# A pre-norm attention and gated-MLP layer on one Trainium2 core: other block choices, another order at the tail

## The chip, the core and the metric

The kernel runs on one core of one Trainium2 chip. A core has a matrix engine (TensorE, in the profile PE, its weight loads PEld), a vector engine (VectorE, DVE), a scalar engine for activation functions (ScalarE, ACT), a general engine (GpSimd, POOL) and a queue that issues transfers (SyncE, SP). Each runs its own instruction stream and they meet through semaphores. The time is device microseconds of one execution. Five runs of the kernel before gave a median of 750.84 us, from 750.54 to 751.12.

## The reference

All tensors are bfloat16; the sequence has 2048 rows of 512.

```python
B, S, D, H = 1, 2048, 512, 32          # Dh = 16, F = 1792
qkv = layernorm(x) @ wqkv              # q, k, v of 32 heads
p = softmax(q @ k.T * 16 ** -0.5)      # per head, 2048 x 2048
h = x + (p @ v) @ wo
g, u = layernorm(h) @ w_gate, layernorm(h) @ w_up
out = h + (sigmoid(g) * u) @ w_down
```

With 16 columns a head, the exponentials (32 x 2048 x 2048) weigh as much as the matmuls.

## The kernel before, in words

**Attention.** A unit is 128 x 512 scores of one head: 256 query columns against two tiles of 128 keys (512 columns against one tile in the first two blocks). The array is used in four parts of 32 rows for the scores, one for each head row j, so that up to four heads are multiplied side by side (`scores`, L1087). A tile is usually three units in three PSUM banks. ScalarE takes the exponential of two or three units in one instruction (L1415). Where three units are there, VectorE can take the third (`dexp_first`, L1258): it turns the score into the bits of a 16-bit float with one operation, and GpSimd makes two shifted copies (L1279), so that three value products are summed for this unit where ScalarE's needs one. Values are multiplied with 17 columns, the last a constant, so each accumulator row also holds the row sum (`av`, L1235). All value products go to PSUM bank 0 (`acc`). When a group of four heads has had all its keys, `finish_group` lets VectorE transpose the sum (L1153), take reciprocals into `rsum` (L1123), scale (L1124) and, for every second group, transpose back into `ot` (L1129).

**The rest.** Projections, output projection with its layer norm (`wo_ln`), gate and up products (`ffn_up`, L826), the tanh that stands for the sigmoid (L856), their product (L898) and the down projection (`ffn_down`, L844) are generators in a queue `bg`. They are called dense work: one step is two to four matmuls.

**The planner.** The order of instructions on all engines is written out by hand while the program is built. A clock T for each engine is carried along: 216 ns for a matmul of 512 columns (`MM`, L638), 112 ns for each change between scores, value products and dense work (`SWITCH`, L639), 51 + 426.5 ns per unit for an exponential (L1416), 601 ns for one of VectorE (L1260), and tails and latencies (L520, L521). For every tile n the loop issues the scores of the next tile, the exponential of this one, and then fills PE until the clock says that the exponential is through (`lim`, L1431). Each block of the filling is chosen by a rule: a step of dense work if there are tokens for it, else value products of up to 12 units, else one dummy matmul that keeps PE's clock up (`stir`), else 100 ns go by.

`PLAN` (L23) overrides the rule, by the key 16 n + step:

- steps 0 to 13 are the blocks of tile n (L1435). 1, 2 or 3: value products of up to 4, 8 or 12 units. 4: a dense step whatever the tokens. 5: let 100 ns go by. 9: end the tile.
- 14 turns the head row of VectorE's unit (L1035).
- 15 decides the sharing (L1398). 1: ScalarE takes all three units. 2: VectorE takes one even where the clock says that it is late.

**The tail.** After the last tile, one block of 256 query rows is left to finish, in a fixed order: value rows of all earlier tiles; on ScalarE a square root to load its table (L1504); 2 matmuls that put twice x into the two output banks `hps` (L1506) and 6 that add the first three quarters of the output projection (L1509); the weights of the 14 last gate and up products, loaded by SP into the freed `J` tiles (L1519, ten transfers); the last value rows and `finish_group` (L1525); the last quarter of the projection (L1532); the layer norm, with 14 matmuls of down projection left over from the queue beside it (`leftover`, L1551); transposes, 10 more such matmuls; 14 rounds of gate, up, tanh and product (`gate_mm`, `tanh_out`, `glu_out`), where gate and up use two pairs of PSUM banks by turns and all tanh results one buffer `th`; 28 matmuls of down projection (L1584), two copies out (L1587) and two stores (L1588).

**The guard.** The exponentials take no row maximum. So at the end VectorE looks whether all row sums lie in a range (L1593 to L1600), one matmul sums the result over the partitions (L1601), and a cast puts it into `flag` (L1603). All engines load the flag (L1607) and branch (L1608): only if a sum is out of range does `general` do everything again in a safe way.

Of the kernel before, what the change touches and what calls it, by code (L numbers as in the profile page):

```python
# [8 lines left out]
FP32 = mybir.dt.float32  # L9
FP16 = mybir.dt.float16  # L10
BF16 = mybir.dt.bfloat16
I16 = mybir.dt.int16
I32 = mybir.dt.int32
I64 = mybir.dt.int64
ALU = mybir.AluOpType
ACT = mybir.ActivationFunctionType
AX = mybir.AxisListType
# [2 lines left out]
DependencyClass = mybir.DependencyClass  # L20
DependencyReason = mybir.DependencyReason

PLAN = {414: 2, 528: 5, 656: 5, 672: 2, 736: 4, 737: 3, 750: 2, 769: 9, 801: 2, 815: 1, 817: 2, 1198: 3, 1200: 3, 1201: 3, 1376: 1, 1409: 3, 1423: 1, 1472: 9, 1473: 5, 1474: 4, 1601: 9, 1634: 3, 1682: 4, 1696: 9, 1713: 4, 1840: 9, 1857: 5, 1872: 4, 1873: 1, 1890: 9, 1938: 1, 2033: 1, 2047: 1, 2144: 5, 2145: 2, 2161: 2, 2384: 2, 2417: 4, 3728: 3, 3730: 4, 4240: 1, 4255: 1, 4321: 3, 4353: 4, 4367: 2, 4752: 2, 4753: 5, 4767: 2, 6112: 5, 6129: 3, 7040: 3, 7041: 3, 7696: 4, 7711: 1, 7713: 4, 7742: 2, 7761: 9, 7904: 2, 8512: 4, 8513: 3, 8913: 1, 8926: 3, 8928: 2, 8930: 1, 8943: 2, 8944: 4, 8960: 3, 8975: 1, 9200: 3, 9393: 4, 9410: 4, 9889: 4, 9890: 3, 9952: 2, 9984: 3, 10000: 2, 10178: 3, 10302: 2, 10528: 3, 10543: 2, 10640: 1, 10687: 2, 10703: 2, 10848: 4, 10894: 2, 10945: 1, 10959: 2, 11023: 1, 11089: 4, 11102: 1, 11103: 1, 11106: 1}  # L23

LOG2E = 1.4426950408889634

# [6 lines left out]
SUM_LOW, SUM_HIGH = 256.0, 60000.0  # L33
# [111 lines left out]
def kernel(  # L145
# [11 lines left out]
    nc = tc.nc  # L157
    P = 128
    S, D = A_x.shape[1], A_x.shape[2]
# [4 lines left out]
    NG = H // 4  # L164
    NP = NG // 2
# [37 lines left out]
    ident2 = const.tile([P, P], BF16)  # L203
# [13 lines left out]
    wo_sb = const.tile([P, NP, D], BF16)  # L217
    rsum = const.tile([P, S // 32 * NG], FP32)
# [31 lines left out]
    fill = prep.tile([P, QC], BF16, name="fill")  # L250
# [186 lines left out]
    for h in range(2):  # L437
# [11 lines left out]
        out=small.tile([P, 1], FP32, name="warm")[:], in_=eps_t[:], func=ACT.Exp))])  # L449
# [29 lines left out]
    while left:  # L479
        best = None  # L480
        for n in left:
# [11 lines left out]
            for eng, ns, fn in t.opts:  # L493
                start = max(at, free[eng])
# [17 lines left out]
    acc = PS[:, 0, :]  # L512
# [9 lines left out]
    T = {e: max(0.0, free[e] - tasks["go"].end) for e in free if e != "N"}  # L522
# [141 lines left out]
    def pe_time(mode, ns, acts=None):  # L664
        st["acts"].append((T["P"], ns / MM * 512 if acts is None else acts))
        T["P"] += ns + (SWITCH if st["mode"] != mode else 0.0)
        st["mode"] = mode
# [89 lines left out]
    OT, otj = {}, {}  # L757
# [79 lines left out]
    def glu_out(hT, f, th, ps):  # L837
        w = ps.shape[-1]
        nc.vector.scalar_tensor_tensor(out=hT[:, f, 0:w], in0=th[:, 0:w], scalar=1.0, in1=ps,  # L839
                                       op0=ALU.add, op1=ALU.mult)  # L840
# [13 lines left out]
    def tanh_out(ps):  # L854
        th = fwork.tile([P, QC], FP32, name="th")
        nc.scalar.activation(out=th[:, 0:ps.shape[-1]], in_=ps, func=ACT.Tanh, scale=0.5)  # L856
        return th
# [160 lines left out]
    N = ahead // GU  # L1018
# [81 lines left out]
    avq = []  # L1100
# [112 lines left out]
    def av(limit, loose=60.0, full=False):  # L1213
        busy = [st["acc"][k] for k in acc_of(*gseq[st["cur"]])[1] if st["acc"][k] is not None]
        if any(j.end is None or j.end + LAT > T["P"] + loose for j in busy):
            return 0
        uns, rows = in_rows(av_ready(loose), ahead_ready(), limit, full)
        if not uns:
            return 0
        T["P"] = max([T["P"]] + [un.end + LAT for un in uns + busy])  # L1220
        for un in uns:
            qc, g, kt, j = un.u
            dst, halves = acc_of(qc, g)
            for k in halves:
                st["acc"][k] = None
            force(("v", kt * SPAN[qc]))
            avq.remove(un)
            c = count[qc, g, j]
            count[qc, g, j] += 1
            todo[qc, g, j] -= 1  # L1230
            h = 8 * (g // 2) + 2 * j + g % 2
            w = CW[qc]
            clears = 0 in halves
            for i in range(SPAN[qc]):
                nc.tensor.matmul(dst[32 * j:32 * j + VW, 0:w], lhsT=un.v[:, kt * SPAN[qc] + i, h, :],  # L1235
                                 rhs=un.ap[:, i * w:(i + 1) * w], start=clears and c + i == 0,
                                 stop=(todo[qc, g, j] == 0 and i == SPAN[qc] - 1), tile_position=(0, 32 * j),
                                 skip_group_check=True)
        pe_time("av", MM * rows + 4 * len(uns), 128 * len(uns))
        for un in uns:  # L1240
            if un.slot is not None:
                un.slot.end = T["P"] + DRAIN
        while st["cur"] < len(gseq) and av_last() == 0:
            finish_group(*gseq[st["cur"]])
            st["cur"] += 1
        return len(uns)
# [126 lines left out]
    xl = xnT[3]  # L1373
# [124 lines left out]
    ends = [PS[:, wide["base"] + i, :] for i in range(3)] + [PS[:, last + i, :] for i in range(3)]  # L1498
    hps, gu = ends[0:n], ends[n:n + 4]
    nc.vector.tensor_scalar(out=ident2[:], in0=ident_bf[:], scalar1=2.0, scalar2=None, op0=ALU.mult)  # L1500
    while any(un.n < N - 1 and un.slot is not None for un in avq):
        flush()
        av(8, 1e12)
    nc.scalar.activation(out=small.tile([P, 1], FP32, name="warm")[:], in_=eps_t[:], func=ACT.Sqrt)  # L1504
    for i in range(n):
        nc.tensor.matmul(hps[i], lhsT=ident2[:], rhs=xl[:, i, :], start=True, stop=False)  # L1506
    for p in range(NP - 1):
        for i in range(n):
            nc.tensor.matmul(hps[i], lhsT=OT[qc, p][:, i * P:(i + 1) * P], rhs=wo_sb[:, p, :],  # L1509
                             start=False, stop=False)  # L1510
    T["P"] += MM * n * NP
    tw = {}
    for i in range(QB):
        t = dvx.tile([P, 3, GQ, QC], I16, name="J", bufs=QB)[:].rearrange("p a b n -> p (a b n)")
# [7 lines left out]
        if len(tw) == FC:  # L1522
            break

    while avq:  # L1525
        flush()
        av(8, 1e12)
    flush()
    mv = small.tile([P, n, nc.vector.BN_AGGR_DIM], FP32, name="mvl")
    rstd = small.tile([P, n], FP32, name="rstdl")  # L1530
    for i in range(n):
# [42 lines left out]
    for job in held:  # L1574
        job.fn()
    hT = fpool.tile([P, FC, PW], BF16, name="hT")
    for f in range(FC):
        g_ps, u_ps = gu[f % 2 * 2], gu[f % 2 * 2 + 1]
        gate_mm(g_ps, tw[f][:, 0], r)
        gate_mm(u_ps, tw[f][:, 1], r)  # L1580
        glu_out(hT, f, tanh_out(g_ps[:, 0:CW[qc]]), u_ps[:, 0:CW[qc]])
    for i in range(n):
        for f in range(FC):
            nc.tensor.matmul(hps[i], lhsT=hT[:, f, i * P:(i + 1) * P], rhs=wd[:, f, :],  # L1584
                             start=False, stop=(f == FC - 1), skip_group_check=True)
        ob = fwork.tile([P, D], BF16, name="ob", bufs=2)
        nc.scalar.activation(out=ob[:], in_=hps[i], func=ACT.Copy, scale=0.5)  # L1587
        nc.sync.dma_start(out=out_v[:, CQ[qc] // P + i, :], in_=ob[:])  # L1588

    bad = small.tile([P, 1], FP32, name="bad")  # L1590
    okay = work.tile([P, S // 32 * NG], FP32, name="xs")
    rs = rsum[:]
    nc.vector.tensor_scalar(out=okay[:], in0=rs, scalar1=2 / SUM_HIGH, scalar2=None, op0=ALU.is_ge)  # L1593
    nc.vector.scalar_tensor_tensor(out=okay[:], in0=rs, scalar=2 / SUM_LOW, in1=okay[:],
                                   op0=ALU.is_le, op1=ALU.mult)
    nc.vector.tensor_reduce(out=bad[:], in_=okay[:], axis=AX.X, op=ALU.min)
    badb = small.tile([P, 1], BF16, name="badb")
    nc.vector.tensor_scalar(out=badb[:], in0=bad[:], scalar1=-1.0, scalar2=1.0, op0=ALU.mult, op1=ALU.add)
    ones1 = small.tile([P, 1], BF16, name="ones1")
    nc.vector.memset(ones1[:], 1.0)  # L1600
    nc.tensor.matmul(acc[0:1, 0:1], lhsT=ones1[:], rhs=badb[:], start=True, stop=True)  # L1601
    flag = const.tile([1, 1], I32, name="flag")
    nc.vector.tensor_copy(out=flag[:], in_=acc[0:1, 0:1])  # L1603
    main.close()
    order_ctx.close()

# [31 lines left out]
```

## Time and profile before

| what | value |
|---|---|
| median of five runs | 750.84 us (750.54 to 751.12) |
| the profiled execution | 750.95 us, its span 749.1 us |
| busy: PE, ScalarE, VectorE, GpSimd | 713.7, 710.6, 617.7, 392.4 us |
| exponentials of VectorE (L1258) | 611, 682 ns busy each |
| three largest idle times of ScalarE, 9 to 100 us | 2.4 us for value products (L1235), 1.3 and 1.1 us for scores (L1087) |
| end of the last exponential | 714.78 us |
| last down projection matmul ends | 743.36 us |

The profile is of one execution. Its span goes from the first to the last instruction of the program; what lies around it makes the rest of the device time. An instruction's row tells its start or its group's count, its length, the line, the engine, what it writes and reads, and what its engine waited for before it. Lines are of the kernel before. Matmuls overlap in the array, as do instructions on ScalarE and VectorE, so distances from start to start say more of an engine's pace than busy times.

### The profile page before, as it was taken

To read this page: it belongs to the slowest core of one execution; us is meant where nothing else is said; L and a number is where in the kernel's file an instruction comes from. 1 tells how busy PE (TensorE), PEld (TensorE's weight loads), DVE (VectorE), ACT (ScalarE), POOL (GpSimd) and SP (SyncE) were. 2 spreads that over 40 slices of the span, in tenths; PEclk is the share of its full clock that TensorE was granted. 3 is DMA by queue.
4 is the path that set the end of the run, shared out by engine and by line. 5 is a ranking of instruction groups with operands and counts; after the bars stand their busy time and mean duration, and the time that the engine had idled before them with its cause. 6 is when DMAs were issued, how large, how long until landed. Compare 5 with 4: busy or idle time off the path is not lost.

```text
span 749.1 us, 27149 instructions
## 1 busy us (share of the span) xinstructions
PE 713.7 (95%) x11497; PEld 346.0 (46%) x11571; DVE 617.7 (82%) x1223; ACT 710.6 (95%) x788; POOL 392.4 (52%) x715
## 2 busy tenths in 40 slices
PE   7999998888999999999999999999999999999986
PEld 3332223444455445544555455535544455455554
DVE  7987898788988888898999678977889778898843
ACT  7988999999999999999999999999999999999952
POOL 2733556666565545655555545555564555566500
PEclk9999999999999999999999999999999999999999
DMA  7000006000132003210122123201321133003350
GB/s 239 0 2 1 1 2 170 2 3 3 31 100 76 21 10 101 87 31 30 44 63 69 37 63 100 62 9 39 101 58 37 31 94 114 10 10 87 101 169 18
DMA packets 68928, 41.65 MB, mean 56 GB/s; under 512 B 3521, under 2 KB 68801, under 8 KB 68801
## 3 DMA queue, kind: packets, MB, share of 16 engines
q1 hardware_dynamic: 68512, 39.59, 17.9%
q8 instruction: 92, 1.51, 0.8%
q14 instruction: 36, 0.29, 0.1%
q10 hardware_dynamic: 288, 0.26, 0.1%
HBM read 37.75 MB, written 2.10 MB: 53 GB/s over the span
## 4 chain that ended last, share of the span: by engine, by line
PE 71%; ACT 17%; DVE 7%; issue 4%; DMA 0%; POOL 0%; DVEq 0%; ACTq 0%; POOLq 0%
PE PS L1087 24%; PE PS L1235 22%; PE PS L826 12%; ACT pt L1415 12%; PE PS L844 6%; DVE J L1258 3%; PE PS L318 2%; PE PS L765 2%; PE PS L313 2%; ACT xnT L1415 2%; ACT pe L1415 1%; ACT th L856 1%; DVE xs L1153 1%; PE PS L1584 1%; ACT xb L1415 1%
## 5 line engine op out<-in xcount | busy, mean ns | idle before, releaser
L1279 POOL INT64_ADD J<-J x646 | 374.1, 592 | 303.4 <-DVE J L1258 260.4
L1415 ACT ACTIVATE pt<-PS 128x1024 f16<-128x1024 f32 (+1 forms) x516 | 520.8, 1120 | 9.2 <-PE PS L1235 4.8
L1258 DVE TENSOR_SCALAR J<-PS 128x512 int16<-128x512 f32 x611 | 408.9, 682 | 76.5 <-PE PS L1087 43.4
L1087 PE MATMUL PS<-QT,KT 32*128 32x256 bf16 (+1 forms) x3712 | 263.8, 276 | 13.6 <-ACT pt L1415 8.0
L1235 PE MATMUL PS<-J,Vaug 128*17 128x256 f16 (+1 forms) x3486 | 238.3, 279 | 2.0 <-DVE xs L1153 1.1
L1235 PE MATMUL PS<-pt,Vaug 128*17 128x256 f16 (+1 forms) x2049 | 195.6, 279 | 1.3 <-DVE xs L1153 1.0
L1087 PEld LDWEIGHTS <-KT 32*128 32x128 bf16 x3840 | 88.7, 92 | 197.7 <-issue 193.7
L1235 PEld LDWEIGHTS <-Vaug 128*17 128x17 bf16 x6164 | 138.5, 90 | 88.1 <-issue 82.4
L826 PE MATMUL PS<-xnT,wgu 128*128 128x256 bf16 x784 | 113.1, 275 | 0.2 <-DVE ob L850 0.2
L1415 ACT ACTIVATE xnT<-PS 128x1024 f16<-128x1024 f32 (+1 forms) x89 | 97.8, 1129 | 0.2
L826 PEld LDWEIGHTS <-wgu 128*128 128x128 bf16 x784 | 63.8, 98 | 38.9 <-issue 33.5
L1235 PE MATMUL PS<-xnT,Vaug 128*17 128x256 f16 x368 | 54.5, 274 | 0.0
L844 PE MATMUL PS<-wd,hT 128*128 128x512 bf16 x171 | 51.7, 383 | 2.3 <-issue 2.2
L1415 ACT ACTIVATE QTb<-PS 128x1024 f16<-128x1024 f32 x42 | 45.8, 1091 | 0.6 <-PE PS L1087 0.6
L856 ACT ACTIVATE th<-PS 128x512 f32<-128x512 f32 (+1 forms) x63 | 38.6, 612 | 7.9 <-DVE hT L839 6.7
L898 DVE SCALAR_TENSOR_TENSOR hT<-th,PS 128x512 bf16<-128x512 f32 x49 | 33.4, 681 | 6.2 <-PE PS L826 6.1
L1153 DVE STREAM_TRANSPOSE xs<-PS 128x256 f32<-128x256 f32 (+1 forms) x60 | 27.7, 462 | 10.8 <-PE PS L1235 10.3
L1235 PE MATMUL PS<-QTb,Vaug 128*17 128x256 f16 (+1 forms) x166 | 27.5, 275 | 0.4 <-DVE xs L1153 0.4
L1415 ACT ACTIVATE xb<-PS 128x1024 f16<-128x1024 f32 (+2 forms) x26 | 26.1, 1034 | 1.9 <-PE PS L1087 1.3
L1124 DVE TENSOR_TENSOR o<-xs,rsum 128x128 bf16<-128x128 f32 (+1 forms) x60 | 24.5, 408 | 2.1
L1415 ACT ACTIVATE pe<-PS 128x1024 f16<-128x1024 f32 (+2 forms) x22 | 21.9, 1068 | 1.5 <-PE PS L1235 0.9
L844 PEld LDWEIGHTS <-hT 128*128 128x128 bf16 x196 | 12.3, 97 | 20.8 <-issue 17.5
(128 smaller groups left out, 394.0 us busy)
## 6 DMA issues: line engine op xcount, KB each, us to landing
wgu<-in_B_w_gate_dram SPq DMA_DIRECT2D x49, 256.0 KB, 3.0
wgu<-in_B_w_up_dram SPq DMA_DIRECT2D x49, 256.0 KB, 3.4
out_dram<-ob SPq DMA_DIRECT2D x16, 128.0 KB, 1.7
wd<-in_B_w_down_dram SPq DMA_DIRECT2D x1, 1792.0 KB, 7.6
xr<-in_A_x_dram SPq DMA_DIRECT2D x14, 128.0 KB, 4.5
xb<-in_A_x_dram SPq DMA_DIRECT2D x6, 256.0 KB, 6.6
J<-in_B_w_gate_dram SPq DMA_DIRECT2D x4, 384.0 KB, 5.4
J<-in_B_w_up_dram SPq DMA_DIRECT2D x4, 384.0 KB, 6.1
```

The source lines that it names most:

```text
L313: nc.tensor.matmul(ps, lhsT=w_sb[:, d, p * P:(p + 1) * P], rhs=xnT[c][:, d, :], start=(d == 0), stop=(d == DC - 1))
L826: nc.tensor.matmul(ps[:, 0:PARTS[r][2]], lhsT=w[:, d, :], rhs=hn_of(r)[:, d, :], start=(d == 0), stop=(d == DC - 1))
L844: nc.tensor.matmul(ps, lhsT=hT[:, f, i * P:(i + 1) * P], rhs=wd[:, f, :], start=(f == 0), stop=(f == FC - 1))
L856: nc.scalar.activation(out=th[:, 0:ps.shape[-1]], in_=ps, func=ACT.Tanh, scale=0.5)
L898: nc.vector.scalar_tensor_tensor(out=hT[:, f:f + k, 0:w], in0=th[f][:].rearrange("p (k n) -> p k n", k=k), scalar=1.0, in1=ps2.rearrange(" ...
L1087: nc.tensor.matmul(pss[:, ui, i * CW[qc]:(i + 1) * CW[qc]], lhsT=KT[g // 2][32 * j:32 * j + 32, k * P:(k + 1) * P], rhs=q[32 * j:32 * j + ...
L1124: nc.vector.tensor_tensor(out=o2[:, 0:w // 32, DH * a:DH * a + DH], in0=xs[:, 0:w // 32, 0:DH], in1=rec.to_broadcast([P, w // 32, DH]), op ...
L1153: j = dve(650 - ns[0], lambda: nc.vector.transpose(out=xs[:, 0:w // 32, :].rearrange("p b r -> p (b r)"), in_=src), Mark(T["P"] + DRAIN), ...
L1235: nc.tensor.matmul(dst[32 * j:32 * j + VW, 0:w], lhsT=un.v[:, kt * SPAN[qc] + i, h, :], rhs=un.ap[:, i * w:(i + 1) * w], start=clears and ...
L1258: nc.vector.tensor_scalar(out=J[:, 0, k, :], in0=src, scalar1=ZOFF, scalar2=float(-min(CHORDS)), op0=ALU.add, op1=ALU.max)
L1279: nc.gpsimd.int64_add(words(s), words(0), CHORDS[s - 1] * (1 + 2 ** 16 + 2 ** 32 + 2 ** 48))
L1415: ex = nc.scalar.activation(out=pt, in_=pss[:, 0:wa, :], func=ACT.Exp, scale=AS)
```

## The change

Three things are edited.

1. `PLAN` is another table: 316 entries where there were 92. Three keys have the same value in both (1423, 8928 and 10703).
2. At the tail, the 2 + 6 matmuls of the output projection become a list `fill`. The loop that finished the earlier value rows ahead of them is gone. One loop now issues value products whenever the planner's clock has them ready within 120 ns, one matmul of `fill` when it hasn't, and what is left of `fill` after the last value rows and the VectorE work of `finish_group`. The table load and the weight loads stand ahead of this loop.
3. The row sum operations go between the last gates: the compare after gate 2, the combined compare after 4, the minimum after 6, the small scaling and the ones after 8, flag matmul and cast after 10. The load of the flag stays at the end.

```diff
-PLAN = {414: 2, 528: 5, 656: 5, 672: 2, 736: 4, 737: 3, 750: 2, 769: 9,
...
+PLAN = {65: 5, 97: 2, 140: 1, 172: 2, 175: 2, 177: 3, 255: 2, 320: 4,
...
-    while any(un.n < N - 1 and un.slot is not None for un in avq):
-        flush()
-        av(8, 1e12)
+    fill = [lambda i=i: nc.tensor.matmul(hps[i], lhsT=ident2[:], rhs=xl[:, i, :], start=True, stop=False)
+            for i in range(n)]
+    fill += [lambda p=p, i=i: nc.tensor.matmul(hps[i], lhsT=OT[qc, p][:, i * P:(i + 1) * P], rhs=wo_sb[:, p, :],
+                                               start=False, stop=False) for p in range(NP - 1) for i in range(n)]
+    fill = deque(fill)
     nc.scalar.activation(out=small.tile([P, 1], FP32, name="warm")[:], in_=eps_t[:], func=ACT.Sqrt)
-    for i in range(n):
-        nc.tensor.matmul(hps[i], lhsT=ident2[:], rhs=xl[:, i, :], start=True, stop=False)
-    for p in range(NP - 1):
-        for i in range(n):
-            nc.tensor.matmul(hps[i], lhsT=OT[qc, p][:, i * P:(i + 1) * P], rhs=wo_sb[:, p, :],
-                             start=False, stop=False)
-    T["P"] += MM * n * NP
...
+    flush()
     while avq:
-        flush()
-        av(8, 1e12)
+        if av(8, 120.0):
+            flush()
+        elif fill:
+            fill.popleft()()
+            pe_time("dense", MM)
+        else:
+            flush()
+            av(8, 1e12)
     flush()
+    while fill:
+        fill.popleft()()
+        pe_time("dense", MM)
...
+    checks = {2: lambda: nc.vector.tensor_scalar(out=okay[:], in0=rs, scalar1=2 / SUM_HIGH, scalar2=None, op0=ALU.is_ge),
+              4: lambda: nc.vector.scalar_tensor_tensor(out=okay[:], in0=rs, scalar=2 / SUM_LOW, in1=okay[:],
+                                                        op0=ALU.is_le, op1=ALU.mult),
+              6: lambda: nc.vector.tensor_reduce(out=bad[:], in_=okay[:], axis=AX.X, op=ALU.min),
+              8: bits}
+    flag = const.tile([1, 1], I32, name="flag")
     for f in range(FC):
         g_ps, u_ps = gu[f % 2 * 2], gu[f % 2 * 2 + 1]
         gate_mm(g_ps, tw[f][:, 0], r)
         gate_mm(u_ps, tw[f][:, 1], r)
         glu_out(hT, f, tanh_out(g_ps[:, 0:CW[qc]]), u_ps[:, 0:CW[qc]])
+        if f in checks:
+            checks[f]()
+        if f == 10:
+            nc.tensor.matmul(acc[0:1, 0:1], lhsT=ones1[:], rhs=badb[:], start=True, stop=True)
+            nc.vector.tensor_copy(out=flag[:], in_=acc[0:1, 0:1])
...
-    nc.tensor.matmul(acc[0:1, 0:1], lhsT=ones1[:], rhs=badb[:], start=True, stop=True)
-    flag = const.tile([1, 1], I32, name="flag")
-    nc.vector.tensor_copy(out=flag[:], in_=acc[0:1, 0:1])
```

`bits` holds the scaling and the fill of ones, as they were.

More of the change, by code (lines that the diff above doesn't have):

```diff
@@ L21 @@
 DependencyReason = mybir.DependencyReason
-PLAN = {414: 2, 528: 5, 656: 5, 672: 2, 736: 4, 737: 3, 750: 2, 769: 9, 801: 2, 815: 1, 817: 2, 1198: 3, 1200: 3, 1201: 3, 1376: 1, 1409: 3, 1423: 1, 1472: 9, 1473: 5, 1474: 4, 1601: 9, 1634: 3, 1682: 4, 1696: 9, 1713: 4, 1840: 9, 1857: 5, 1872: 4, 1873: 1, 1890: 9, 1938: 1, 2033: 1, 2047: 1, 2144: 5, 2145: 2, 2161: 2, 2384: 2, 2417: 4, 3728: 3, 3730: 4, 4240: 1, 4255: 1, 4321: 3, 4353: 4, 4367: 2, 4752: 2, 4753: 5, 4767: 2, 6112: 5, 6129: 3, 7040: 3, 7041: 3, 7696: 4, 7711: 1, 7713: 4, 7742: 2, 7761: 9, 7904: 2, 8512: 4, 8513: 3, 8913: 1, 8926: 3, 8928: 2, 8930: 1, 8943: 2, 8944: 4, 8960: 3, 8975: 1, 9200: 3, 9393: 4, 9410: 4, 9889: 4, 9890: 3, 9952: 2, 9984: 3, 10000: 2, 10178: 3, 10302: 2, 10528: 3, 10543: 2, 10640: 1, 10687: 2, 10703: 2, 10848: 4, 10894: 2, 10945: 1, 10959: 2, 11023: 1, 11089: 4, 11102: 1, 11103: 1, 11106: 1}
+PLAN = {65: 5, 97: 2, 140: 1, 172: 2, 175: 2, 177: 3, 255: 2, 320: 4, 332: 1, 368: 3, 400: 3, 428: 2, 432: 2, 449: 1, 450: 4, 560: 1, 572: 2, 625: 2, 639: 2, 657: 4, 688: 2, 735: 1, 751: 2, 768: 3, 848: 5, 896: 4, 960: 3, 988: 1, 990: 1, 1054: 1, 1056: 3, 1073: 9, 1120: 2, 1153: 5, 1168: 5, 1185: 2, 1217: 1, 1249: 9, 1324: 1, 1340: 2, 1360: 1, 1409: 9, 1423: 1, 1564: 1, 1630: 1, 1681: 9, 1682: 5, 1697: 4, 1711: 2, 1713: 9, 1724: 1, 1729: 1, 1740: 1, 1792: 9, 1808: 9, 1809: 1, 1840: 2, 1868: 2, 1872: 9, 1889: 5, 1919: 2, 1938: 3, 1950: 3, 1952: 5, 1970: 5, 1984: 4, 2000: 9, 2018: 4, 2033: 4, 2076: 2, 2080: 9, 2096: 9, 2128: 2, 2140: 2, 2172: 1, 2192: 1, 2194: 4, 2240: 4, 2256: 5, 2288: 3, 2304: 4, 2305: 1, 2321: 1, 2400: 4, 2498: 9, 2562: 9, 2624: 3, 2656: 5, 2668: 2, 2704: 4, 2736: 1, 2784: 3, 2785: 3, 2796: 1, 3025: 4, 3026: 2, 3058: 9, 3164: 2, 3167: 1, 3280: 2, 3297: 5, 3356: 1, 3360: 2, 3393: 4, 3487: 1, 3503: 2, 3567: 1, 3568: 4, 3600: 4, 3664: 2, 3696: 2, 3729: 4, 3792: 4, 3822: 1, 4012: 2, 4047: 2, 4065: 3, 4096: 2, 4112: 2, 4113: 5, 4159: 2, 4188: 2, 4193: 4, 4208: 3, 4220: 2, 4224: 3, 4239: 1, 4273: 4, 4288: 3, 4289: 3, 4380: 1, 4385: 1, 4402: 5, 4416: 3, 4496: 2, 4544: 2, 4592: 2, 4655: 1, 4769: 1, 4864: 9, 4945: 9, 4972: 2, 4976: 2, 5004: 1, 5054: 2, 5072: 5, 5120: 1, 5151: 1, 5153: 9, 5154: 2, 5182: 3, 5183: 2, 5218: 9, 5248: 5, 5308: 1, 5312: 2, 5344: 2, 5360: 3, 5361: 2, 5362: 3, 5436: 2, 5468: 1, 5504: 3, 5534: 2, 5536: 1, 5568: 4, 5598: 1, 5599: 2, 5632: 1, 5633: 4, 5644: 2, 5664: 3, 5666: 5, 5695: 1, 5728: 4, 5777: 4, 5793: 5, 5810: 9, 5825: 3, 5826: 1, 5840: 1, 5888: 9, 5900: 2, 5952: 2, 5966: 1, 5980: 1, 6018: 9, 6034: 9, 6047: 2, 6065: 2, 6082: 4, 6111: 1, 6124: 2, 6128: 2, 6156: 1, 6222: 3, 6239: 2, 6268: 1, 6284: 1, 6305: 4, 6306: 3, 6369: 3, 6370: 3, 6384: 1, 6524: 2, 6528: 3, 6544: 2, 6592: 3, 6673: 4, 6688: 3, 6705: 9, 6720: 3, 6766: 2, 6767: 2, 6846: 2, 6847: 2, 6881: 9, 6928: 3, 6929: 9, 6930: 1, 6962: 3, 7020: 1, 7057: 2, 7090: 1, 7136: 2, 7152: 2, 7164: 1, 7166: 1, 7169: 3, 7170: 4, 7182: 3, 7201: 4, 7262: 1, 7394: 3, 7408: 3, 7436: 2, 7440: 4, 7458: 2, 7473: 3, 7474: 9, 7554: 9, 7660: 1, 7727: 1, 7841: 5, 7856: 3, 7873: 5, 7888: 1, 7906: 3, 7934: 3, 7953: 2, 7998: 3, 8064: 3, 8112: 2, 8160: 3, 8176: 2, 8208: 4, 8225: 1, 8257: 1, 8270: 2, 8366: 3, 8384: 4, 8428: 1, 8770: 9, 8784: 1, 8895: 1, 8928: 2, 8992: 3, 9120: 1, 9152: 1, 9196: 1, 9216: 4, 9217: 4, 9232: 3, 9250: 9, 9407: 1, 9420: 2, 9454: 3, 9490: 2, 9506: 4, 9516: 1, 9532: 1, 9584: 3, 9596: 1, 9612: 2, 9615: 1, 9664: 2, 9697: 4, 9792: 3, 10016: 4, 10031: 2, 10129: 3, 10130: 1, 10236: 1, 10238: 2, 10316: 1, 10338: 9, 10399: 2, 10418: 3, 10494: 3, 10544: 1, 10652: 2, 10657: 1, 10672: 2, 10703: 2, 10748: 2, 10768: 9, 11007: 1, 11020: 1, 11038: 1, 11039: 2, 11040: 1, 11054: 3, 11073: 4, 11088: 4, 11106: 2, 11121: 9}
@@ L1576, with bits @@
     hT = fpool.tile([P, FC, PW], BF16, name="hT")
+    bad = small.tile([P, 1], FP32, name="bad")
+    okay = work.tile([P, S // 32 * NG], FP32, name="xs")
+    badb = small.tile([P, 1], BF16, name="badb")
+    ones1 = small.tile([P, 1], BF16, name="ones1")
+    rs = rsum[:]
+    def bits():
+        nc.vector.tensor_scalar(out=badb[:], in0=bad[:], scalar1=-1.0, scalar2=1.0, op0=ALU.mult, op1=ALU.add)
+        nc.vector.memset(ones1[:], 1.0)
+    checks = {2: lambda: nc.vector.tensor_scalar(out=okay[:], in0=rs, scalar1=2 / SUM_HIGH, scalar2=None, op0=ALU.is_ge),
[4 more added lines that the diff above has]
+    flag = const.tile([1, 1], I32, name="flag")
     for f in range(FC):
@@ L1588 @@
         nc.sync.dma_start(out=out_v[:, CQ[qc] // P + i, :], in_=ob[:])
[L1590 to L1600, printed above, removed]
-    nc.tensor.matmul(acc[0:1, 0:1], lhsT=ones1[:], rhs=badb[:], start=True, stop=True)
-    flag = const.tile([1, 1], I32, name="flag")
-    nc.vector.tensor_copy(out=flag[:], in_=acc[0:1, 0:1])
     main.close()
```

## The prediction

> **What bounds the kernel now.** I read the share of busy time first, then the same by stretch, then who waits for whom, and last the chain and the order of instructions of the last 37 us. The page and a table of stretches (length, then busy us and count of PE, PEld, DVE, ACT, POOL, then clock, DMA share, GB/s):
>
> ```profile
> PE 713.7 (95%) x11497; PEld 346.0 (46%) x11571; DVE 617.7 (82%) x1223; ACT 710.6 (95%) x788; POOL 392.4 (52%) x715
> 9.00:100.00 91.00, 85.52 (x708) 27.86 (x721) 77.61 (x149) 83.66 (x90) 44.33 (x78) 1.00 0.09 27
> 100.00:275.00 175.00, 162.73 (x2893) 76.97 (x2909) 150.98 (x292) 171.15 (x185) 103.79 (x180) 1.00 0.15 44
> 275.00:500.00 225.00, 220.24 (x3870) 111.64 (x3886) 189.99 (x379) 222.88 (x242) 123.49 (x216) 1.00 0.20 58
> 500.00:714.00 214.00, 211.30 (x3805) 108.75 (x3826) 180.00 (x347) 213.68 (x234) 118.94 (x204) 1.00 0.22 63
> ```
>
> From 9 to 714 us ScalarE, which takes most exponentials, is busy 691.4 of 705 us: it sets the pace of the main loop. Busy time flatters it, because its instructions overlap: a 128x1024 exponential is busy 1120 ns on the page, but in the trace the next one starts 904 ns after it where nothing is late (1330 ns for 128x1536, 477 ns for a tanh of 512). Against these intervals the starts of ScalarE in the main loop lose 30.2 us in sum: 3.6 us in slips under 0.05 us, 9.4 us in 77 slips up to 0.25 us, and 17.2 us in 32 stalls over 0.25 us. By stretch those 32 cost 9.4, 4.4, 2.7 and 0.4 us, dense early and almost none after 500. PE is not the bound all the time either: a score group of six matmuls takes 0.330 us at best and 0.362 us on average until PE's next group starts, over 596 groups, which is 19 us of slack.
>
> The chain of waits around the end of the loop, and rows of the order of instructions (start, length, what):
>
> ```profile
> 713.63 1.20 PE PS L1235 x36
> 714.83 0.54 PE PS L1506 x2
> 715.37 1.29 PE PS L1509 x6
> 716.66 0.36 PE PS L1235 x6
> ...
> 718.10 0.46 DVE ot L1129
> 718.55 0.27 issue
> 718.82 0.38 PE PS L1532
> ```
>
> ```profile
> 713.18 1.60 ACT L1415 ACTIVATE xnT<-PS 128x1536 f16<-128x1536 f32 x1
> ...
> 718.82 0.38 PE L1532 MATMUL PS<-wo_sb,ot 128*128 128x512 bf16 x1 [1.83 <-DVE ot L1129]
> ...
> 737.68 0.39 ACT L856 ACTIVATE th<-PS 128x256 f32<-128x256 f32 x1 [0.55 <-DVE hT L839]
> 738.10 0.42 DVE L839 SCALAR_TENSOR_TENSOR hT<-th,PS 128x256 bf16<-128x256 f32 x1 [0.51 <-ACT th L856]
> 738.44 0.42 DVE L1593 TENSOR_SCALAR xs<-rsum 128x512 f32<-128x512 f32 x1
> 738.89 0.69 DVE L1594 SCALAR_TENSOR_TENSOR xs<-rsum,xs 128x512 f32<-128x512 f32 x1
> 739.62 0.69 DVE L1596 TENSOR_REDUCE bad<-xs 128x1 f32<-128x512 f32 x1
> ```
>
> The last exponential ends at 714.78. PE then does eight matmuls of the output projection (L1506, L1509) before the six last value rows (L1235), and afterwards stands 1.83 us while VectorE turns and normalizes what those rows made. Behind L1532 PE is full to 743.36. The end itself, by the lines of the flag's load and branch (count, shortest/median/longest ns, first and last start):
>
> ```profile
> L1607 PEldq TENSOR_LOAD <-flag x1: 494/494/494, 743.7 to 743.7; - x1
> L1608 PEldq COMPARE_BRANCH  x1: 3392/3392/3392, 744.3 to 744.3; - x1
> L1608 SPq COMPARE_BRANCH  x1: 45/45/45, 745.3 to 745.3; - x1
> ```
>
> PE's branch ends at 747.65 and the closing barriers at 749.1 follow it. SP's own waits would be through at 746.2.
>
> **Last value rows first.** The same instructions in another order: 2 + 6 matmuls at 0.216 us from start to start, 1.83 us in all (714.76 to 716.59). Now the value rows can start at 714.84, just after the last exponential, and L1532 follows their start by 2.23 us as before (716.59 to 718.82). Within that time PE does the six rows (0.36 us) and the eight matmuls (1.83 us), 2.19 us, so they fit. L1532 starts at 717.07: **-1.75 us**. If the planner's clock takes the rows for late and issues all eight matmuls first, it is 0; if VectorE were slower it could not be more than 1.83. The square-root table load (714.79, 1.28 us, then 0.20 us) ends at 716.3, ahead of its user, so it stays hidden. What is late next is nothing but PE: the 14 matmuls of L844 behind L1532 (3.02 us) cover the layer norm as now. The moved step also puts the ten loads of gate weights on SP ahead of the last value rows in program order. They wait for readers of the J tiles; the last is issued at 715.52 now, lands near 717.2, and the first gate reads at 724.83, some 723.1 after the change. Even 2 us later nothing waits, and SP's next work, an output at 723.92, is behind none of it. Without that cover each us past 5.9 costs one.
>
> **Row sums between the last gates.** Off the end go nothing but PE's flag matmul and the cast: the five VectorE operations at 738.44 to 740.5 stand beside the down projection today. Between the gates they meet a ping-pong: tanh, product, tanh share one th buffer, every 0.933 us, while PE needs 8 x 0.111 = 0.89 us, so that at the fourteenth gate PE is only about 0.2 us away from waiting for a PSUM bank. VectorE is free for 0.51 us in each turn. The 0.42 us compare fits; the two of 0.69 us do not. [...] Taken with full busy times that is 2 x (0.69 + 0.03 - 0.51) = 0.42 us late, less the 0.2 us: +0.22 us. The trace says that the queue is in order but overlaps: 738.10 to 738.44 is 0.34 us for a product busy 0.42, and the 611 operations of L1258, busy 0.682, start 0.608 apart. So one turn takes 0.34 + 0.61 = 0.95 instead of 0.933 and the loss is near 0.04 us in two turns. I take +0.1 us. The flag matmul and its weights among the gates have no row of that kind; at the end they cost PE 0.09 us beyond a usual interval (742.966 to 743.274, against 0.216), while a change of tile shape elsewhere shows 0.21 us idle of PEld; bounds 0 and 0.3, taken at 0.1 (nearer to its own row). The result of the VectorE part is ready about 734.5 and PE reaches the matmul about 734.6, so no wait; were it late, the gates behind it would wait as long. Sum **+0.2 us**. The fill of ones and the small scaling (0.06 and 0.16 us) and the cast (0.14 us) fit into the 0.51 us.
>
> **The end.** With the flag in place, PE's load of it no longer waits for matmul and cast (743.27 to 743.62): it can start near 743.25 instead of 743.66. **-0.4 us** (0 to -0.65, the latter if it need not wait for the last matmul to drain). This counts only because PE's branch is last. [...]
>
> **The choices.** PLAN goes from 92 to 316 entries, only three of them the same. In the four stretches (a tile is about 1.015 us) 17, 23, 16 and 36 become 43, 79, 121 and 73. They move three kinds of thing: the order of blocks on PE, the head row, and who takes the exponential (15 entries on that become 34). The work on PE, ACT and DVE is otherwise the same. Their worth cannot be summed by instruction; it is bounded. The most is every stall over 0.25 us, 17.2 us, and then some slips. The least: entries for short value blocks (1 or 2) rise from 21 to 121; eight matmuls take 0.338 us and 24 take 0.775, so splitting costs 0.12 us a block, 100 x 0.12 = 12 us of PE if nothing hides it. The planner's clocks speak for the upper side: 51 + 426.5 per unit gives 904 and 1330.5, just the measured intervals; 216 a dense matmul, 112 a switch (score group 328 against 330), 601 for a VectorE exponential against 608. Choices made by these clocks should hold on the chip, though small errors add over 695 tiles. I take a quarter of the 17.2 us: **-4.3 us**. PE must have the room, and its 19 us has it.
>
> Sum against the profiled span: 749.1 - 1.75 + 0.2 - 0.4 - 4.3 = 742.85. The profiled execution took 750.95, 1.85 more than its span, and the median is 0.11 under that: 742.85 + 1.85 - 0.11 = **744.6 us**.
>
> **The rivals.** *Only the tail gains.* The old stalls go, others come: 750.84 - 1.95 = 748.9. For it: 19 of 32 stalls lie in the first 100 us, where projections and loads crowd PE whatever the choices. Against it: the clocks fit well. *The value rows don't move*: fills are issued first, choices give nothing, 750.84 - 0.2 = 750.6; the last exponential and the last rows of PE end within 0.1 us of each other now, so a small error of the clock decides. *Short blocks make PE the bound*, the slower side: of the 12 us, half comes through after 275 us, where ScalarE has lost little and PE is busy 98%: 750.84 + 6 - 1.95 = 754.9. It decides once more than 3.5 of the 12 us show without stalls recovered. *Most stalls go*: two thirds of 17.2 and the tail, 750.84 - 11.5 - 1.95 = 737.4.
>
> **How the numbers follow.** Likeliest case (740 to 748) 0.53, only the tail 0.15, unmoved 0.08, short blocks 0.17, most stalls 0.07. A measurement tells about 0.2%, 1.5 us, from no change: faster is under 749.3. Faster: 0.53 + 0.07 + two thirds of 0.15 = 0.70; same: the rest of 0.15 and most of 0.08, 0.12; slower: 0.18. The range leaves out the best case's end and the worst of short blocks: 738 to 754; the likeliest case's own range is 740 to 748.
>
> **What would show it.** Right: the last value rows ahead of the eight matmuls and no 1.83 us gap at the last projection; PE's flag load right behind the last down matmul, its branch still some 3.4 us; a tanh interval near 0.95 twice; ScalarE's lost 30.2 us down by four or so, mostly before 275 us. Wrong: more, shorter L1235 groups with ScalarE's idle before 714 grown, a later last exponential, or another number of VectorE exponentials than 611, each of which moves 0.43 us of ScalarE's work and two more value rows onto PE.

## The result, and the profile after

The changed kernel takes 750.20 us in the median of 25 runs (746.55 to 751.07), the kernel before 750.77 in 46 (750.45 to 752.08). The ratio is 0.9981, 95% interval 0.9974 to 0.9987. That is 0.2% faster, 0.57 us by the medians and 1.4 us by the ratio, where 6.25 us were forecast. The prediction called faster what lies under 749.3; by that line the median is no change, though 11 of the 27 executions below lie under it. The table of stretches and the page's first row, of the changed kernel, columns as before:

```profile
PE 707.9 (95%) x11472; PEld 347.9 (47%) x11545; DVE 614.0 (82%) x1216; ACT 712.6 (96%) x789; POOL 384.3 (52%) x695
9.00:100.00 91.00, 84.65 (x685) 27.08 (x695) 75.24 (x145) 86.15 (x91) 40.20 (x70) 1.00 0.09 28
100.00:275.00 175.00, 161.19 (x2906) 76.99 (x2929) 149.52 (x292) 172.28 (x186) 103.55 (x176) 1.00 0.15 44
275.00:500.00 225.00, 219.96 (x3927) 113.97 (x3938) 192.32 (x380) 224.37 (x245) 120.92 (x206) 1.00 0.20 59
500.00:712.00 212.00, 207.28 (x3736) 108.81 (x3756) 178.34 (x342) 210.94 (x230) 117.72 (x204) 1.00 0.22 64
```

ScalarE stands less early on, but it is busy longer in all: 712.6 us where it was 710.6. GpSimd has 626 copy instructions instead of 646. The page's group of VectorE's exponentials says why:

```profile
L1258 DVE TENSOR_SCALAR J<-PS 128x512 int16<-128x512 f32 x602 | 402.9, 683 | 76.1 <-PE PS L1087 40.6
```

602, where there were 611. The chain of waits at the end:

```profile
710.94 2.01 PE PS L1235 x60
712.95 0.16 issue
713.11 0.38 PE PS L1501
713.49 1.29 PE PS L1503 x6
714.78 0.43 PE PS L1537 x2
715.21 3.02 PE PS L844 x14
718.23 0.61 PE PS L307 x8
718.84 3.02 PE PS L844 x14
721.87 9.61 PE PS L826 x88
731.47 0.09 PE PS L1605
731.57 2.73 PE PS L826 x24
734.29 0.05 issue
734.35 6.00 PE PS L1609 x27
```

The value rows (L1235) are ahead of the projection (L1501, L1503), the last projection (L1537) follows without the gap, and the flag matmul (L1605) costs PE 0.09 us among the gates. The 14 matmuls of L844 after the transposes were 10 before: the new choices leave four more to the tail. The load of the flag and the branch of PE:

```profile
L1618 PEldq TENSOR_LOAD <-flag x1: 487/487/487, 736.3 to 736.3; - x1
L1619 PEldq COMPARE_BRANCH  x1: 3652/3652/3652, 736.9 to 736.9; - x1
L1619 SPq COMPARE_BRANCH  x1: 45/45/45, 741.4 to 741.4; - x1
```

PE's branch runs from 736.9 to 740.55, beside the last down projection, and ends the kernel no longer.

**One execution is not like the next.** This profiled execution took 747.04 us (span 745.1), 3.2 us under the median, and its mean granted PE clock is 1.000. Of 27 executions for which the clock is recorded, six have 1.000 and take 746.55 to 747.04; five have 0.998 and take 748.03 to 748.57; sixteen have 0.992 to 0.995 and take 749.58 to 751.07. (One stretch of 3.413 us at half clock lowers the mean over 745 us by 0.0023.) So there are two questions: why the change is worth only 4.0 us of span at full clock (749.1 to 745.1), and what takes 3 us back in most executions.

### The profile page after: what moved, and what is told of

Read it like the earlier page. It is cut to its first block, busy times and chain, and to the rows that moved or that the text cites. A ratio compares the mean times of both kernels' runs of the same rounds, so it can differ in the third digit from the quotient of the medians.

```text
span 745.1 us, 26993 instructions
## 1 busy us (share of the span) xinstructions
PE 707.9 (95%) x11472; PEld 347.9 (47%) x11545; DVE 614.0 (82%) x1216; ACT 712.6 (96%) x789; POOL 384.3 (52%) x695
## 4 chain that ended last, share of the span: by engine, by line
PE 65%; ACT 22%; DVE 7%; issue 4%; POOL 1%; DMA 0%; DVEq 0%; ACTq 0%; POOLq 0%
PE PS L1087 22%; PE PS L1235 20%; ACT pt L1415 15%; PE PS L826 11%; PE PS L844 6%; PE PS L313 3%; ACT xnT L1415 3%; DVE J L1258 2%; ACT th L856 1%; DVE st L273 1%; PE PS L765 1%; ACT QTb L1415 1%; PE PS L318 1%; PE PS L1609 1%; DVE Vaug L322 1%
## 5 line engine op out<-in xcount | busy, mean ns | idle before, releaser
L1415 ACT ACTIVATE pt<-PS 128x1024 f16<-128x1024 f32 (+2 forms) x515 | 522.6, 1152 | 4.0 <-PE PS L1087 2.5
L1279 POOL INT64_ADD J<-J x626 | 365.9, 597 | 304.6 <-DVE J L1258 258.7
L1258 DVE TENSOR_SCALAR J<-PS 128x512 int16<-128x512 f32 x602 | 402.9, 683 | 76.1 <-PE PS L1087 40.6
L1087 PE MATMUL PS<-QT,KT 32*128 32x256 bf16 (+1 forms) x3712 | 262.0, 276 | 17.2 <-ACT pt L1415 9.4
L1235 PE MATMUL PS<-J,Vaug 128*17 128x256 f16 (+1 forms) x3453 | 233.8, 279 | 3.1 <-DVE xs L1153 2.3
L1235 PE MATMUL PS<-pt,Vaug 128*17 128x256 f16 (+1 forms) x2055 | 198.0, 279 | 0.9 <-DVE xs L1153 0.9
L1235 PEld LDWEIGHTS <-Vaug 128*17 128x17 bf16 x6142 | 138.6, 90 | 81.9 <-issue 73.8
L1235 PE MATMUL PS<-xnT,Vaug 128*17 128x256 f16 x364 | 55.9, 274 | 0.0
L844 PE MATMUL PS<-wd,hT 128*128 128x512 bf16 x169 | 50.1, 383 | 3.3 <-issue 3.2
L856 ACT ACTIVATE th<-PS 128x512 f32<-128x512 f32 (+1 forms) x63 | 40.6, 644 | 8.8 <-DVE hT L839 5.0
L1235 PE MATMUL PS<-QTb,Vaug 128*17 128x256 f16 (+1 forms) x166 | 29.1, 275 | 0.0
L1415 ACT ACTIVATE pe<-PS 128x1024 f16<-128x1024 f32 (+1 forms) x25 | 26.0, 1095 | 1.3 <-PE PS L1087 1.3
L1124 DVE TENSOR_TENSOR o<-xs,rsum 128x128 bf16<-128x128 f32 (+1 forms) x60 | 22.6, 376 | 2.1
L844 PEld LDWEIGHTS <-hT 128*128 128x128 bf16 x196 | 13.0, 97 | 21.0 <-issue 15.8
```

What stands on the lines that cost most here:

```text
L844: nc.tensor.matmul(ps, lhsT=hT[:, f, i * P:(i + 1) * P], rhs=wd[:, f, :], start=(f == 0), stop=(f == FC - 1))
L1087: nc.tensor.matmul(pss[:, ui, i * CW[qc]:(i + 1) * CW[qc]], lhsT=KT[g // 2][32 * j:32 * j + 32, k * P:(k + 1) * P], rhs=q[32 * j:32 * j + ...
L1124: nc.vector.tensor_tensor(out=o2[:, 0:w // 32, DH * a:DH * a + DH], in0=xs[:, 0:w // 32, 0:DH], in1=rec.to_broadcast([P, w // 32, DH]), op ...
L1258: nc.vector.tensor_scalar(out=J[:, 0, k, :], in0=src, scalar1=ZOFF, scalar2=float(-min(CHORDS)), op0=ALU.add, op1=ALU.max)
L1279: nc.gpsimd.int64_add(words(s), words(0), CHORDS[s - 1] * (1 + 2 ** 16 + 2 ** 32 + 2 ** 48))
L1415: ex = nc.scalar.activation(out=pt, in_=pss[:, 0:wa, :], func=ACT.Exp, scale=AS)
```

## The experiments

**Theories.** A count of the matmul columns that PE takes in any 3.413 us shows where the kernels differ. (A dense matmul of 512 columns counts 512, the four-part ones a quarter of their columns. The weight loads are counted, because some matmul records are missing: the profile of before has 11571 loads and 11497 matmuls. The 3.413 us are the length of a piece of half clock, seen below in pieces of 3.41 us, and the 217th part of the 740.69 us that the changed kernel's trace spends at full clock. Starts are 50 ns apart.) The kernel before never falls under 2560, at 21 us; at 125 us it has 2688. The changed one falls to 1920 at 39.6, 2304 at 125.2 and 2048 at 142.1 us. Starts of such a span that see fewer than 3000 columns fill some 0.6 us of the kernel before and 5.4 us of the changed one. One such stretch in both, and the 3.4 us behind it, in the two profiled executions (length, PE busy and count, clock, DMA share, GB/s; before, then changed):

```profile
39.60:43.10 3.50, 3.35 (x19) 1.00 0.01 2
39.60:43.10 3.50, 1.80 (x13) 1.00 0.00 0
43.10:46.50 3.40, 3.40 (x24) 1.00 0.00 0
```

The *clock theory*: PE's clock is halved for some 3.4 us behind such a stretch, in some executions and not in others. The rivals: the tail's edits cost the clock; or the time varies for another reason.

### The changed kernel again

> The changed kernel once more, nothing edited, for a second trace of it. Clock theory: PE does too little in three stretches (around 40, 125 and 142 us of the span), and in most executions its clock is halved for some 3.4 us behind one, two or three of them, at some 1.5 us each; a trace with a mean clock under 1.0 shows half clock there and nowhere else before the end, and a time of 748 to 751; one with 1.000 shows 746.5 to 747. Rival, the tail: the half clock lies after 700 us. Rival, no clock: the time varies at a clock of 1.000.

No edit. 749.83 us in the median of 10 runs (747.22 to 751.07). The traced one took 748.20 us at 0.998. PE's stretches around 40 us, in the same columns, and PE's own order there:

```profile
39.70:43.10 3.40, 1.70 (x11) 1.00 0.00 0
43.10:46.50 3.40, 3.40 (x19) 0.50 0.00 0
```

```profile
40.11 0.61 PE L318 MATMUL PS<-wv_sb,xnT 128*128 128x512 bf16 x2
41.72 0.39 PE L1087 MATMUL PS<-QT,KT 32*128 32x512 bf16 x3 [1.00 <-DVE xnT L720]
42.81 0.39 PE L1087 MATMUL PS<-QT,KT 32*128 32x512 bf16 x2 [0.70 <-ACT xb L1415]
43.13 1.03 PE L717 MATMUL PS<-ident_bf,xn 128*128 128x128 bf16 x8
43.96 1.06 PE L318 MATMUL PS<-wv_sb,xnT 128*128 128x512 bf16 x2
44.96 0.61 PE L1087 MATMUL PS<-QT,KT 32*128 32x512 bf16 x3
```

PE waits 1.00 us for a copy of VectorE and 0.70 us for an exponential; then, from 43.1 to 46.5 us, its clock is 0.50 and eight transposes take 1.03 us where they take 0.62 at full clock. ScalarE's lost time grows by 1.4 us (25.6 against 24.2). That is what the clock theory says, and half clock stands nowhere else up to the end of PE's work.

### The tail alone, the choices alone

```diff
 tail alone, to the changed kernel          choices alone, to the kernel before
-PLAN = (the new table)                     -PLAN = (the old table)
+PLAN = (the old table)                     +PLAN = (the new table)
```

> The tail's two edits with the old choices. From the two traces the tail is worth 1.76 (value rows first) - 0.17 (gates) + 0.99 (end) = 2.6 us. Clock theory: 748.2 us, within 0.5 us in all runs, clock as before. Rival, the tail costs the clock: as scattered as the changed kernel, 747 to 751.

> The new choices with the old tail. At full clock 1.4 us faster than before, 749.4. Clock theory: this kernel has the scatter, 749.4 to 753.5, with its median near 752.5, slower than before by 1.5 to 2 us. Rival, the tail costs the clock: 749.4 in all runs.

| kernel | median (range), runs | ratio to before, 95% interval | clock |
|---|---|---|---|
| tail alone | 748.12 (747.84 to 748.86), 5 | 0.9963 (0.9950 to 0.9976) | 0.999 to 1.000 |
| choices alone | 751.48 (749.75 to 754.03), 12 | 1.0010 (0.9997 to 1.0024) | 0.991 to 0.998 |

The tail gives 2.8 us (2.6 expected) and does not scatter. The choices bring the scatter. At their highest clock, 0.998, they take 749.75 to 750.32, 0.6 to 1.1 us under before (1.4 expected). Their trace, at 0.996, has one piece of half clock, from 43.2 to 46.6, and half clock in its last 2.8 us, where PE's matmuls are over. Their median is 0.6 us over before rather than the 1.5 to 2 expected, and the interval of the ratio includes no change. Together: a tail that gains, and a table that gains at full clock and gives it back in the median.

### Unused matmuls in the thin stretches

```diff
+    WARM_AT = {28: 1, 29: 1, 113: 1, 130: 1, 131: 1}
+    def keep_up(n):      # clocks of the planner untouched
+        for _ in range(WARM_AT.get(n, 0)):
...
+            nc.tensor.matmul(PS[:, 1 + (st["ring"] + 1) % st["R"], :], lhsT=wo_sb[:, 0, 0:P], rhs=wo_sb[:, 0, :],
+                             start=True, stop=True)
...
             T["P"] += 100
+        keep_up(n)
         run_dve(hor)
```

> The changed kernel with five unused matmuls of 128x512 (0.22 us each) in PE's idle time of those three stretches (two near 40, one near 128, two near 144 us); the planner's clocks don't count them, so nothing else moves. Clock theory: mean clock 1.000 in every run, 746.5 to 747.2, faster than before by 0.5%. Rival, the clock falls elsewhere or for another reason: the scatter stays, median 750.2.

747.15 us (746.74 to 747.46), 5 runs; ratio 0.9948, 0.9935 to 0.9961. The fewest columns in 3.413 us are now 2816, and the starts under 3000 fill 0.95 us. PE's order in the same stretch:

```profile
41.00 0.38 PE L672 MATMUL PS<-wo_sb 128*128 128x512 bf16 x1
42.19 0.39 PE L1098 MATMUL PS<-QT,KT 32*128 32x512 bf16 x3 [0.81 <-DVE xnT L731]
42.79 0.38 PE L672 MATMUL PS<-wo_sb 128*128 128x512 bf16 x1 [0.21 <-DVE Vaug L322]
43.28 0.39 PE L1098 MATMUL PS<-QT,KT 32*128 32x512 bf16 x2
```

The unused matmuls (L672) stand in waits that were there anyway, and ScalarE's lost time is that of the changed kernel at full clock. Five matmuls more, 3 us less: this version beats both kernels. The mean clock was not 1.000 in every run but 0.998 to 1.000. The trace, at 0.999, has half clock in its last 1.0 us alone, where PE has nothing left to do. The runs at 0.998 are as fast as the others (746.74 to 747.15), so a mean that is lower by 0.002 is not by itself a loss; where it stood in them was not traced.

### Which stretch

```diff
-    WARM_AT = {28: 1, 29: 1, 113: 1, 130: 1, 131: 1}
+    WARM_AT = {28: 1, 29: 1}                 # early only
+    WARM_AT = {113: 1, 130: 1, 131: 1}       # late only
```

> The changed kernel with only the two unused matmuls near 40 us. Clock theory: the stretches at 125 and 142 us still do too little, so one or two halvings are left: 747 to 750, up to some 3 us of scatter, and a trace with half clock between 125 and 147 us. Rival, only the stretch near 40 counts: 747.2 in all runs.

> The changed kernel with only the three unused matmuls near 128 and 144 us. Clock theory: at most one halving is left, behind 40 us: 747 or 748.5, none above 749. Rival, only the stretch near 40 counts: the scatter stays, up to 751.

With the early stretch filled: 747.07 (746.81 to 748.27), 5 runs, three at 1.000, one at 0.999, one at 0.998; the trace fell on a full clock and shows no place. With the late ones filled: 748.61 (747.00 to 749.62), 9 runs, one at 1.000, six at 0.998, two at 0.996 and 0.994. So the stretch at 40 us costs a halving in most executions; that the later ones add theirs is seen in one trace below. The bound "none above 749" was missed by two runs. Five further traces of the changed kernel, and one of the kernel with the late stretches filled, were to place the second halving.

> One more trace of the changed kernel, for the place of a second and third halving. Clock theory: with a mean clock of 0.995 or less, half clock stands behind more than one of the stretches at 40, 125 and 142 us. Rival: it stands longer behind 40 us and nowhere else.

> A further trace of the changed kernel. Clock theory: a mean clock of 0.995 or less goes with half clock behind more than one of the stretches at 40, 125 and 142 us. Rival: it stands longer behind 40 us and nowhere else.

> A further trace of the changed kernel. If its mean clock is 0.995 or less: three-places theory, half clock behind 40, 125 and 142 us in separate pieces of 3.4 us; one-place theory, one piece of 6.8 or 10.2 us behind 40 us.

> A further trace of the changed kernel. If its mean clock is 0.995 or less: three-places theory, half clock behind 40, 125 and 142 us in separate pieces of 3.4 us; one-place theory, one piece of 6.8 or 10.2 us behind 40 us.

> A further trace of the changed kernel. If its mean clock is 0.995 or less: three-places theory, half clock behind 40, 125 and 142 us in separate pieces of 3.4 us; one-place theory, one piece of 6.8 or 10.2 us behind 40 us.

> A second trace of the kernel with the unused matmuls near 128 and 144 us only. Three-places theory: half clock behind 40 us at most, one piece of 3.4 us, 747 or 748.5 us. One-place theory: with a mean clock under 0.997 a longer piece behind 40 us, 749 us or more.

Four of the five took 748.22 to 748.43 us with one piece of half clock of 3.41 us, starting between 42.9 and 43.7. The fifth took 750.23 at 0.995. Its stretches of PE:

```profile
44.80:48.20 3.40, 3.40 (x11) 0.50 0.00 0
143.80:147.20 3.40, 2.04 (x40) 0.99 0.03 7
147.20:150.60 3.40, 3.40 (x52) 0.50 0.00 0
```

Two pieces behind two thin stretches, so not one place. They start 102.40 us apart, which is 30 times 3.413 us. The trace with the late ones filled had one piece only, from 44.5 to 47.9, and 749.04 us: 2 us over its one run at 1.000, of which some 0.4 may belong to the session, in which the kernel before took 751.19. In the changed kernel a single piece goes with 1.2 to 1.4 us. What the run of 749.62 at 0.994 lost is open, and half clock behind the stretch at 125 us was seen in no trace.

### The same in the kernel before

```diff
     def stir():
...
-        nc.tensor.matmul(PS[:, 1 + (st["ring"] + 1) % st["R"], :], lhsT=wo_sb[:, 0, 0:P], rhs=wo_sb[:, 0, :],
-                         start=True, stop=True)
         pe_time("dense", MM)
```

> The kernel before with its 18 unused matmuls (L658) left out, while the planner's clocks still count them, so nothing else moves. Clock theory: the stretch at 22 us falls from 2560 matmul columns to 1664 and those at 125, 142 and 154 us to some 2500, so the kernel before gets the same scatter, 750.8 to 752.5 with a clock under that of before in most runs. Rival, the clock doesn't hang on such matmuls: 750.8, or less by what PE no longer does.

752.25 us (750.24 to 757.50), 10 runs; ratio 1.0034, 1.0009 to 1.0059; clock 0.986 to 0.999, the longest times at the lowest clocks. In its trace:

```profile
22.20:25.60 3.40, 1.89 (x16) 0.99 0.00 0
25.60:29.00 3.40, 3.40 (x16) 0.51 0.01 2
```

Leaving out 18 matmuls whose results nobody reads made the old kernel slower (750.76 us in that session with them). The direction was foreseen, the reach was not: up to 6.7 us, though only one stretch fell under 2400 columns. Under 3000 there are eight of them between 20 and 188 us, and the starts under 3000 fill 7.1 us in its trace. The runs of 756.63 to 757.50 themselves were not traced.

### The tail in two

```diff
 the kernel before, with either
+ fill list and the one loop (value rows first), or
+ checks between the gates (guard early)
```

> Of the tail only the order of value rows and output projection, with the old choices and the old place of the row sum check. From the traces: 1.76 us off, 749.1 us. Rival, the fill matmuls only move a wait: 750.8.

> Of the tail only the row sum check between the gates, with the old choices and the old order of value rows. From the traces: 0.17 us more at the gates, 0.99 less at the end because PE's flag load and its branch of 3.4 to 3.7 us run ahead of the last down projection: 0.8 us off, 750.0 us. The prediction's step (a branch that starts 0.4 us earlier) would give 0.2 off, 750.6.

Value rows first: 749.27 (748.88 to 750.46), 11 runs; ratio 0.9980, 0.9971 to 0.9989: 1.6 us. Guard early: 749.87 (749.52 to 751.26), 11 runs; ratio 0.9989, 0.9980 to 0.9998: 0.2 to 1.5 us, 1.0 by the medians, beside 0.8 from the traces and 0.2 by the prediction's step. The interval hardly parts the two; the trace does, since PE's branch starts there at 739.9 and ends at 743.3, ahead of the last store's issue at 744.0:

```profile
L1614 PEldq COMPARE_BRANCH  x1: 3359/3359/3359, 739.9 to 739.9; - x1
```

The sum of the two halves is the tail's 2.8 within what the intervals allow.

### No table at all

```diff
-PLAN = (the new table)
+PLAN = {}
```

> The changed kernel with an empty table, so that the rule alone orders the blocks. It says what both tables are worth beside it: the old one gives 748.1 with this tail, the new one 746.9 at full clock. The theory that each table gains by fewer stalls of ScalarE says that this one has more than 30 us of them and takes 750 to 758; that the number of VectorE exponentials matters as much says that the loop's end follows from stalls plus 0.43 us for every unit fewer on VectorE.

753.76 us (753.47 to 755.13), 5 runs; ratio 1.0036, 1.0022 to 1.0050. With the same tail the old table is worth 5.6 us (753.76 to 748.12), the new one at full clock 6.6 us from the rule's own full-clock times (753.5 to 746.9), of which the clock takes 3. The loop's end can be booked under two terms, the time that ScalarE loses against its own pace, and 0.4265 us for each unit that VectorE doesn't take (the planner's figure; from start to start ScalarE takes 904 ns for two units and 1330 for three). (The trace without a table has a piece of half clock from 114.2 to 117.6 us, whose loss is in its first term.)

| kernel | VectorE units | ScalarE's lost us | of it over 0.25 us | last exponential ends |
|---|---|---|---|---|
| before | 611 | 30.2 | 17.2 | 714.78 |
| changed, full clock | 602 | 24.2 | 12.4 | 712.50 |
| no table | 619 | 38.5 | 24.2 | 720.10 |

From before to changed: -6.0 + 9 x 0.4265 = -2.2; seen -2.28. From before to no table: +8.3 - 8 x 0.4265 = +4.9; seen +5.3. The lost time is taken from the same traces, so this is bookkeeping that closes, not a test; that the nine units cost what it gives them was not tried alone.

## Why the prediction was right or wrong

**Value rows first: right.** -1.75 said. From the end of the last exponential to the weight load of the last projection it was 714.78 to 718.59, and is 712.50 to 714.54: -1.77; alone, 1.6 us. The table load stayed hidden (its last row ends at 714.01), the loads of gate weights too.

**Row sums between the gates: right, a little dear.** +0.2 said, +0.12 seen (from the first gate to the first down matmul 12.36 and 12.48 us). VectorE's rows of the changed kernel:

```profile
726.57 0.42 DVE L839 SCALAR_TENSOR_TENSOR hT<-th,PS 128x256 bf16<-128x256 f32 x1 [0.51 <-ACT th L856]
726.91 0.68 DVE L1592 SCALAR_TENSOR_TENSOR xs<-rsum,xs 128x512 f32<-128x512 f32 x1
727.51 0.42 DVE L839 SCALAR_TENSOR_TENSOR hT<-th,PS 128x256 bf16<-128x256 f32 x1
```

A turn of 0.94 us (726.57 to 727.51) where full busy times one behind the other (0.42 + 0.03 + 0.69) would have given some 1.14. The distances from start to start told more than the busy times.

**The end: right that the branch was last, wrong in size.** The step "it can start near 743.25 instead of 743.66" gave -0.4, at most -0.65. From the last copy out to the end of the span it was 743.38 to 749.1, and is 740.37 to 745.1: -0.99. PE's sequencer did not wait until the matmuls ahead were done: it loaded the flag at 736.3, some 4 us before the last of them ended (740.34), so the whole branch is hidden, and what ends last now is the output, issued at 741.0 and landed 2.9 us later. The bound was taken from a drain that the load did not need, and the sign "flag load right behind the last down matmul" did not come true.

**The choices: the stalls right, the work wrong.** The quarter of the stalls over 0.25 us, -4.3, is close to what came: 17.2 to 12.4, -4.8. The step that failed here is "the work on PE, ACT and DVE is otherwise the same". Nine units went from VectorE to ScalarE, +3.84 us on the engine that sets the pace, and four down matmuls more in the tail, 4 x 0.216 = +0.86 (14 took 3.02 us where 10 had taken 2.16). The prediction named a changed number of VectorE exponentials among its signs, but costed it at nothing. The sum at full clock: -1.77 + 0.12 - 0.99 - 2.28 + 0.86 = -4.06, beside -4.0 of the spans. The span at full clock, 745.1, is 2.25 us over the forecast 742.85.

**The clock: not in the sum at all.** Here the other step failed, and it is the larger part of the miss, 3.2 us beside some 2.9 of the choices: "PE must have the room, and its 19 us has it". The prediction gave PE its slack as room, and asked only whether PE could be late. It did not ask what happens when PE has too little to do, though the code of before carries the answer (`quiet` and `stir`). Entries 5 and 9 of the table, which rose from 14 to 51, let time go by or end a tile before that branch is reached: tiles 130 and 131, near 142 us, now begin with a 9, and the unused matmuls of before at 140.2, 142.5 and 146.4 us are gone. At 40 us that is not the cause. Neither kernel has an unused matmul between 26 and 126 us, and the new entries of tiles 25 to 28 are 1 to 4; which of the other choices thinned PE's work there is open. The trace of before said so little of it because its clock is 1.00 in every stretch. What the clock takes is the way from 747.0 to 750.2, the rest of the miss. Of the rivals, "short blocks make PE the bound" was wrong in its mechanism: the loss came from PE's doing too little, not from its load (five matmuls more took 3 us off). The gain has the sign that was forecast and a tenth to a quarter of its size, and lies short of the prediction's own line for faster. The rival "the value rows don't move" named 750.6, close to the median by luck: the rows moved, and gained 1.6 us alone.

## What to carry to other kernels

Choices made by a model of the clocks can gain what the model prices and pay with what it doesn't: here the activity with which the matrix engine's clock stayed up (747.15 us with five unused matmuls, 750.20 without). The balance between two engines counts beside the stalls: nine units gave back 3.84 of the 6.0 us that ScalarE no longer lost. When times of one kernel lie in steps instead of around a value, set the granted clock beside each of them before explaining the median. Here a load and a branch at the end of the program ran ahead of the matmuls still queued on their engine (load at 736.3 us, matmuls to 740.34), once the value that they wait for was made early.

## What the runs showed of the hardware that was not expected

Half clock came in pieces of 3.41 us. Eleven of the eighteen traces have one before the end, twelve pieces in all. In every trace the times at which the clock changes, that of the half clock at the end included, lie whole multiples of 3.413 us apart (11, 205, 217 and so on), so each trace shows a grid; a stretch of 3.413 us on it is called a window here. The window just before a piece held 1920 to 2944 columns, and PE was busy 1.70 to 2.04 of 3.4 us in the stretches shown. Of 3619 other windows at full clock, between 9 and 700 us, five held 2304 to 2624, the rest 2944 or more. The lowest of the five is in the profiled execution of the changed kernel itself, from 38.6 to 42.0 us, and cost nothing. Counted 0.2 us earlier, the windows ahead of a piece hold 1664 to 2944, one other 2944, and all the rest 3072 or more. So no piece stood behind an idle window: the thinnest ahead of one still held 1920 columns. A limit near 3000 in this count is an estimate fitted to these traces: the 0.2 us were picked because they part the windows best, and a quarter for a four-part matmul is a guess of what it weighs.

The number of halvings fits as well. If the grid falls at random against the instructions, 5.4 us of starts under 3000 in windows of 3.413 us make an estimated 1.6 halvings in an execution; the clocks of the 27 executions, read as none at 1.000, one at 0.998, two at 0.995 and three at 0.992 or 0.993, make 1.7. In the traces the same instructions lost no piece (747.04 us), one (748.20 to 748.43) or two (750.23); three were seen in none.

PE's compare-and-branch took 3.34 to 3.90 us in the eighteen traces, against 0.05 to 0.07 on the other engines. It cost nothing where it started at 736.9 and ended at 740.55, while the last store landed at 743.9.
